# A two-branch attention kernel: last-token queries and keys in whole kilobytes, early stores of first operands, and the tail's products in other PSUM banks

## The chip, the cores and the metric

The kernel runs on one core of a Trainium2 chip. The metric is the device time of one execution in microseconds (us). The kernel before takes 1713.68 us (median of 3 runs, 1711.49 to 1714.44). All runs told here are timed beside runs of the kernel before on the same chip. The chip was not always the same: e1 to e4 ran on one, e5 to e11 on a second, e12 on a third, e13 and e14 on a fourth, so between these groups the ratios to before are compared, not the times alone.

## The reference, cut to what matters

Two attentions over the same x (2048 tokens of 576) are mixed by a gate.

```python
def _A_ref(x, mem0, Wq, Wk, Wv, Wo, seg_len):      # 32 heads of 128, segments of 32, memory of 8
    mem = mem0
    for s in range(n_seg):                          # 64 segments, one after the other
        h = jnp.concatenate([mem, xs], axis=1)      # 40 tokens: memory, then the segment
        ...                                         # q, k, v from h; masked softmax; o
        mem = o[:, :M, :].copy()                    # the next segment needs this
        outs.append(o[:, M:, :])
...
g = _sigmoid((x * gate_w).sum(-1, keepdims=True))
a = _A_ref(x, A_mem0, A_Wq, A_Wk, A_Wv, A_Wo, A_seg_len)
b = _B_ref(x, B_wqkv, B_wo)                         # ordinary attention over 2048 tokens, 32 heads of 18
return g * a + (1 - g) * b
```

Attention A is a chain of 64 segments. Attention B, "the big attention", has no such order and is worked off in steps before and between the segments.

## The kernel before

The program has three parts. In the **front** x is transposed, B's first queries and keys are projected, A's weights are loaded, and the "last tokens" are projected: the last 8 of each segment's 40 tokens do not depend on the memory, so their q, k and v are made for 16 segments at once, stored to DRAM (qld, kld, vld) and read back by segment.

```python
def last_tokens(q, share, k=None):                  # one group of 16 segments
    ...
    store = nc.sync if share else nc.gpsimd
    xlb = fil.tile([P, NF + 2, P], BF16, name="xlb", bufs=1)
    nc.sync.dma_start(out=xlb[:, :, :].rearrange("p c t -> p (c t)"), in_=xld[q])
    for b in range(HD // 512):                      # 8 blocks of values
        ...                                         # matmuls into pv
        vl = fil.tile([P, 512], BF16, name="vl")    # fil: two buffers
        copy_out(vl[:, :], pv[:, :], share)
        store.dma_start(out=vld[q * P:(q + 1) * P, b * 512:(b + 1) * 512], in_=vl[:, :])
    for w, dstd in ((wq, qld), (wk, kld)):          # 8 blocks of queries, 8 of keys
        ...
                store.dma_start(                    # 16 runs of 64 B in each of 128 rows
                    out=dstd[q].rearrange("p (s f) -> p s f", s=SG)[:, :, 4 * b * LO:4 * (b + 1) * LO],
                    in_=vl[:, :].rearrange("p (s f) -> p s f", s=SG),
                )
```

In the **loop** each segment first loads its last tokens (`v_sb` from vld, `xl` from qld and kld, copied into place by GpSimd). In the **tail** the last group of A's rows is written and the 16 row blocks of the result are finished, each in two half blocks.

```python
def bank(k, shape, dtype, name):                    # three tiles of one PSUM bank each
    if k is None:
        k = turns[0] % 3
        turns[0] += 1
    return ps_a.tile(shape, dtype, name=name, tag=f"b{k}")

def finish(n):
    ...
    for d0 in (0, Dm // 2):                         # two half blocks
        po = bank(None, [P, 512], FP32, "po")
        ...                                         # 5 matmuls into po, then ScalarE in place
        nc.scalar.activation(out=po[:, 0:Dm // 2], in_=po[:, 0:Dm // 2], func=ACT.Copy, scale=omg[:, n:n + 1])
        nc.vector.scalar_tensor_tensor(..., in1=po[:, 0:Dm // 2], op0=ALU.mult, op1=ALU.add)
```

So the product of a half block goes from TensorE to ScalarE to VectorE in the same PSUM tile, and three such tiles are used in turn.

The softmax here doesn't subtract the row's maximum and nothing guards it: scores larger than these inputs give would overflow.

## Time and profile before

| Profiled run (span 1706.9 us) | us |
|---|---|
| first segment's projections start | 234.57 |
| from there to the first final product's ScalarE step | 1430.6 |
| from there to the end | 41.7 |
| TensorE busy | 1494.8 (88%) |

The three times add up to the span; every run below is split at the same two marks (first record of the segment projections; first ScalarE step of the final products), which I call **front**, **loop** and **tail**. The loop is bound by TensorE. The front has holes in which the engines wait for a DMA for most of the time, and the tail ends in a chain of small stores. The prediction below shows the lines that carry this.

### The profile page before, as it was taken

The page shows a single profiled execution, that of the slowest core. Times are in us where ns is not written, and L with a number is a line of the kernel's source. Part 1 is how long each engine was busy: PE and PEld are TensorE (multiplying, and loading weights), DVE is VectorE, ACT ScalarE, POOL GpSimd, SP SyncE. Part 2 cuts the span into 40 slices and gives each one's busy share as a digit, 9 for nine tenths or more (in the row PEclk, how much of TensorE's full clock was granted, in tenths as well). Part 3 has the DMA queues.
Part 4 walks back from the last instruction along what each step waited for, and adds up shares of the span by engine and source line. Part 5 has one row for each costly group of instructions (what it writes and reads, how often), then busy time and mean ns, then how long its engine had stood idle before and what let it go on. Part 6 is the DMA issues. An engine that isn't in the chain of part 4 may idle for free. (4 is left out here: it accounts for less than half of the span.)

```text
span 1706.9 us, 57602 instructions
## 1 busy us (share of the span) xinstructions
PE 1494.8 (88%) x25082; PEld 789.3 (46%) x25082; DVE 963.4 (56%) x2360; ACT 1138.6 (67%) x976; POOL 364.6 (21%) x716
## 2 busy tenths in 40 slices
PE   6476669989999899999999999999999989899986
PEld 3232434445555444454555444555554444444444
DVE  2133245666666566656666656666666656565654
ACT  2154335767777676766776767777777787887873
POOL 5211111122222112131313121322221212120221
PEclk9788879999999999999999999999999999999998
DMA  7875431212221111121212111121211111111133
GB/s 191 277 266 185 106 63 33 58 35 46 50 51 45 43 37 52 44 48 35 59 38 56 42 43 47 46 47 36 58 42 48 33 46 32 45 32 31 30 103 103
DMA packets 127464, 114.38 MB, mean 67 GB/s; under 512 B 62531, under 2 KB 115011, under 8 KB 125619
## 3 DMA queue, kind: packets, MB, share of 16 engines
q1 hardware_dynamic: 106395, 59.03, 13.0%
q0 software_dynamic: 19872, 49.38, 10.9%
q8 instruction: 196, 3.21, 0.8%
q10 hardware_dynamic: 944, 2.29, 0.4%
q14 instruction: 57, 0.47, 0.1%
HBM read 60.94 MB, written 36.10 MB: 57 GB/s over the span
## 5 line engine op out<-in xcount | busy, mean ns | idle before, releaser
L257 ACT ACTIVATE etb<-sb 128x2048 bf16<-128x2048 f32 x512 | 959.5, 1874 | 420.2 <-PE sb L238 420.2
L752 DVE CAST tm<-pvv 128x512 bf16<-128x512 f32 x384 | 264.1, 688 | 170.5 <-PE pvv L740 169.1
L740 PEld LDWEIGHTS <-ht 128*32 128x32 bf16 x7680 | 187.0, 97 | 184.3 <-DVE ht L876 12.6
L238 PE MATMUL sb<-qch,kch 32*128 32x512 bf16 x2048 | 204.8, 389 | 55.6 <-ACT etb L257 36.9
L222 PE MATMUL ob<-etb,vch 128*32 128x512 bf16 x2048 | 206.8, 394 | 5.4 <-DVE tq L159 5.1
L835 DVE CAST ot<-pso 128x320 bf16<-128x320 f32 x256 | 120.3, 487 | 124.3 <-PE pso L823 120.5
L629 PE MATMUL acc<-wo,ot 128*32 128x384 bf16 (+1 forms) x4096 | 158.9, 291 | 5.4 <-DVE ot L835 3.6
L740 PE MATMUL pvv<-wq_m,ht 128*32 128x512 bf16 x2048 | 135.9, 386 | 12.6 <-DVE ht L876 7.1
L740 PE MATMUL pvv<-wk_m,ht 128*32 128x512 bf16 x2048 | 134.4, 383 | 0.0
L740 PE MATMUL pvv<-wv_m,ht 128*32 128x512 bf16 x2048 | 134.1, 382 | 0.0
L238 PEld LDWEIGHTS <-kch 32*128 32x128 bf16 x2048 | 61.7, 91 | 146.5 <-issue 111.4
L685 POOL DMA_DIRECT2D a_dram<-rl x192 | 95.9, 534 | 140.3 <-DVE rl L681 136.5
L629 PEld LDWEIGHTS <-ot 128*32 128x32 bf16 x4096 | 104.6, 97 | 45.8 <-DVE ot L835 11.6
L842 POOL COPY otl<-ot 128x256 bf16<-128x256 bf16 x64 | 27.1, 424 | 392.6 <-DVE ot L835 358.9
L222 PEld LDWEIGHTS <-vch 128*32 128x32 bf16 x2048 | 52.7, 93 | 123.7 <-issue 117.3
L293 DVE CAST vl<-pv 128x512 bf16<-128x512 f32 x96 | 65.9, 686 | 73.7 <-DMA qld<-vl 18.6
L823 PE MATMUL pso<-et,v_sb 64*128 64x40 bf16 x2048 | 82.0, 179 | 22.7 <-DMA v_sb<-tm 11.8
L811 ACT ACTIVATE lt<-pss 128x320 f32<-128x320 f32 x128 | 55.9, 437 | 68.0 <-PE pss L807 58.0
L823 PEld LDWEIGHTS <-v_sb 64*128 64x128 bf16 x2048 | 62.9, 93 | 72.5 <-issue 49.0
L767 PE MATMUL pt<-ident,tm 128*128 128x128 bf16 x1024 | 95.7, 221 | 0.8 <-DVE tm L752 0.8
L640 DVE CAST hl<-acc 128x384 bf16<-128x384 f32 (+1 forms) x128 | 57.7, 451 | 56.2 <-PE acc L629 55.9
L775 DVE COPY kt<-pt 128x512 bf16<-128x512 bf16 x128 | 53.8, 420 | 63.0 <-PE pt L767 63.0
(136 smaller groups left out, 1886.9 us busy)
## 6 DMA issues: line engine op xcount, KB each, us to landing
v_sb<-tm SPq DMA_DIRECT2D x512, 32.0 KB
wo<-in_A_Wo_dram POOLq DMA_DIRECT2D x4, 1152.0 KB, 8.1
vgd<-vt SPq DMA_DIRECT2D x32, 128.0 KB
wv_m<-in_A_Wv_dram POOLq DMA_DIRECT2D x4, 1024.0 KB, 8.1
wq_m<-in_A_Wq_dram POOLq DMA_DIRECT2D x4, 1024.0 KB, 8.2
wk_m<-in_A_Wk_dram POOLq DMA_DIRECT2D x4, 1024.0 KB, 9.1
v_sb<-vld SPq DMA_DIRECT2D x128, 32.0 KB
xl<-qld SPq DMA_DIRECT2D x64, 64.0 KB
```

What stands on the lines that cost most here:

```text
L222: nc.tensor.matmul(ob[32 * j:32 * j + 32, :], lhsT=vc[:, o + 32 * j:o + 32 * j + 32], rhs=et4[:, j, :], start=(kb == 0), stop=(kb == NKB - 1),
L238: nc.tensor.matmul(sb[:, j, :], lhsT=kc[32 * j:32 * j + 32, o:o + P], rhs=qch[gq][32 * j:32 * j + 32, :], start=True, stop=True, tile_posi ...
L257: nc.scalar.activation(out=before[:, :, :], in_=sb[:, :, :], func=ACT.Exp, scale=scale_b)
L293: nc.vector.tensor_copy(out=out, in_=in_)
L629: nc.tensor.matmul(acc[32 * j:32 * j + 32, 0:d1 - d0], lhsT=o[:, h, 0:CT], rhs=wo[:, h, d0:d1], start=(b == 0 and i == 0), stop=(b == 1 an ...
L640: nc.vector.tensor_copy(out=hl[:, 0, d0:d1], in_=acc[:, 0:d1 - d0])
L685: nc.gpsimd.dma_start(out=rows4[m, seg - LO:seg, i * n:(i + 1) * n], in_=rl[32 * i + m * LO:32 * i + (m + 1) * LO, :],)
L740: nc.tensor.matmul(pv[32 * j:32 * j + 32, :], lhsT=ht[:, cc, :], rhs=rw, start=(c == 0), stop=(c == NF), tile_position=(0, 32 * j),)
L752: nc.vector.tensor_copy(out=sbt[x][:, :], in_=ps[x][:, :])
L767: nc.tensor.transpose(out=pt[:, which, :, :, :].rearrange("p j (u i) t -> p j u i t", i=4)[:, :, :, i, :], in_=sbt[x][:, i * Dh:(i + 1) * Dh],
L823: nc.tensor.matmul(pso[:, i * L:(i + 1) * L], lhsT=v_sb[64 * jj:64 * jj + 64, b * 1024 + i * Dh:b * 1024 + (i + 1) * Dh], rhs=et[64 * jj:6 ...
L835: nc.vector.tensor_copy(out=ot[:, j * HG:(j + 1) * HG, :].rearrange("p h t -> p (h t)"), in_=ps["o", b, jj][:, 0:W8],)
```

## The change

Its intent is to close the holes of the front, to make the stores of last-token queries and keys cheaper at the price of reading small pieces ahead of time, and to let the 32 final half blocks run without a break.

```diff
-    qld = dpool.tile([n_seg // SG, P, SG * H * LO], BF16, name="qld")
+    qld = dpool.tile([n_seg // SG, H // 4, P, SG * 4 * LO], BF16, name="qld")
 ...                                       # kld likewise
-                store.dma_start(out=dstd[q].rearrange(...)[...], in_=vl[:, :].rearrange(...))
+                store.dma_start(out=dstd[q, b], in_=vl[:, :])
+                if w is wk and b == H // 4 - 1:
+                    load_xlb(q + 1)                   # the next group's tokens, a group ahead
 ...                                       # in the loop over the four blocks t of x:
+        if t == 0:
+            load_xlb(0)
+        if t < NQC - 1:
+            in_turn(next(pieces))                     # one weight piece between x blocks
         for blk in FIRST:
             project_qk(blk, t, 2)
+        if t == NQC - 1:
+            for blk in FIRST:
+                store_qk(blk, (0,))                   # before the last value projections
 ...
+    load_first()                                      # B's first operands
+    ready.extend([first_loads[-1]] * 2)               # the other weights wait for them
+    for d in pieces:
+        in_turn(d)
 ...                                       # in the loop of segments:
+            if name == "S1" and s + 1 < n_seg:
+                load_qk(s + 1)                        # 64 B pieces, a segment ahead
 ...                                       # finish(n):
-            po = bank(None, [P, 512], FP32, "po")
+            po = pf[:, (2 * n + (d0 > 0)) % 4, :]
 ...                                       # tail: group rows before the products
+    pf = ps_bs.tile([P, 4, QC], FP32, name="sb")      # one tile of four banks
+    g0 = group_span(1, 0)
+    g1 = group_span(2, 1)
+    gr = group_rows(0, n_seg - 1)
+    g0()
+    g1()
+    gl = group_last(1, n_seg - 1)
+    finish(0)
+    gr()
+    gl()
+    for n in range(1, 6):
+        finish(n)
 ...
```

The big attention's score tile, four banks wide, is free by then; the final products take its place. Half of the last group's twelve small stores go to the sync queue.

More of the change, by code (lines that the diff above doesn't have):

```diff
@@ L88 @@
     xld = dpool.tile([n_seg // SG, P, (NF + 2) * P], BF16, name="xld")
-    qld = dpool.tile([n_seg // SG, P, SG * H * LO], BF16, name="qld")
-    kld = dpool.tile([n_seg // SG, P, SG * H * LO], BF16, name="kld")
+    qld = dpool.tile([n_seg // SG, H // 4, P, SG * 4 * LO], BF16, name="qld")
+    kld = dpool.tile([n_seg // SG, H // 4, P, SG * 4 * LO], BF16, name="kld")
     aw1 = ctx.enter_context(tc.tile_pool(name="aw1", bufs=1))
@@ L197, in load_kv @@
             vch[g, kc] = bint.tile([P, KC * P], BF16, name="vch", bufs=6)
-            loads.dma_start(
+            first_loads[:] = [loads.dma_start(
                 out=vch[g, kc][:, :].rearrange("p (k f) -> p k f", f=P),
                 in_=vgd[kc * KC:(kc + 1) * KC, :, g * P:(g + 1) * P].rearrange("k p f -> p k f"),
-            )
+            )]
         def load_q(i):
@@ L260, in b_steps @@
         late.extend(divisions(ob, GB * NQC - 1))
-        while late:
-            late_part()
-    loads = nc.sync
+    loads, first_loads = nc.sync, []
     bgen = b_steps()
@@ L293, in copy_out, with load_xlb @@
             nc.vector.tensor_copy(out=out, in_=in_)
+    xlbs = {}
+    def load_xlb(q):
+        if q < n_seg // SG:
+            xlbs[q] = fil.tile([P, NF + 2, P], BF16, name="xlb", bufs=1)
+            nc.sync.dma_start(out=xlbs[q][:, :, :].rearrange("p c t -> p (c t)"), in_=xld[q])
     def last_tokens(q, share, k=None):
@@ L299, in last_tokens @@
         store = nc.sync if share else nc.gpsimd
-        xlb = fil.tile([P, NF + 2, P], BF16, name="xlb", bufs=1)
-        nc.sync.dma_start(out=xlb[:, :, :].rearrange("p c t -> p (c t)"), in_=xld[q])
+        xlb = xlbs.pop(q)
         for b in range(HD // 512):
@@ L328, in last_tokens @@
                 )
-                store.dma_start(
-                    out=dstd[q].rearrange("p (s f) -> p s f", s=SG)[:, :, 4 * b * LO:4 * (b + 1) * LO],
-                    in_=vl[:, :].rearrange("p (s f) -> p s f", s=SG),
-                )
+                store.dma_start(out=dstd[q, b], in_=vl[:, :])
+                if w is wk and b == H // 4 - 1:
+                    load_xlb(q + 1)
                 yield
@@ L455 @@
     FIRST = (0, 4, 5)
+    pieces = [(w, src) for w, src in ((wv, A_Wv), (wq, A_Wq), (wk, A_Wk))]
+    pieces = (d for w, src in pieces for d in load_weights(w, src))
     for t in range(NQC):
@@ L463 @@
         )
+        if t == 0:
+            load_xlb(0)
+        if t < NQC - 1:
+            in_turn(next(pieces))
         for blk in FIRST:
             project_qk(blk, t, 2)
+        if t == NQC - 1:
+            for blk in FIRST:
+                store_qk(blk, (0,))
         for kb in range(4 * t, 4 * t + 4):
             project_vb(0, kb, 2)
-    for blk in FIRST:
-        store_qk(blk, (0,))
-    for w, src in ((wv, A_Wv), (wq, A_Wq), (wk, A_Wk)):
-        for d in load_weights(w, src):
-            in_turn(d)
+    load_first()
+    ready.extend([first_loads[-1]] * 2)
+    for d in pieces:
+        in_turn(d)
     pgs = ps_bo.tile([P, NT], FP32, name="pgs", tag="ob")
@@ L499, in between @@
             b_advance(1)
-    load_first()
     for blk in FIRST:
@@ L684, in rest @@
                 for m in range(4):
-                    nc.gpsimd.dma_start(
+                    eng = nc.sync if s3 == n_seg - 1 and m % 2 else nc.gpsimd
+                    eng.dma_start(
                         out=rows4[m, seg - LO:seg, i * n:(i + 1) * n],
@@ L974, in load_last @@
     def load_last():
+        while late:
+            late_part()
         nc.vector.memset(wol, 0.0)
@@ L1012, in finish, with load_qk @@
         nc.sync.dma_start(out=out_td[n * P:(n + 1) * P, :], in_=ofin[n])
+    xls = []
+    def load_qk(s):
+        sq, si = divmod(s, SG)
+        w = 4 * LO
+        for srcd in (qld, kld):
+            xl = seg2.tile([P, H, LO], BF16, name="xl")
+            nc.sync.dma_start(
+                out=xl[:, :, :].rearrange("p (b h) t -> p b (h t)", h=4),
+                in_=srcd[sq, :, :, si * w:(si + 1) * w].rearrange("b p f -> p b f"),
+            )
+            xls.append(xl)
+    load_qk(0)
     for s in range(n_seg):
@@ L1016 @@
             put_x(s + 1)
-        sq, si = divmod(s, SG)
         for jj in range(2):
@@ L1023 @@
             )
-        for dst, srcd in ((qt, qld), (kt3, kld)):
-            xl = seg2.tile([P, H, LO], BF16, name="xl")
-            nc.sync.dma_start(
-                out=xl[:, :, :].rearrange("p h t -> p (h t)"), in_=srcd[sq, :, si * H * LO:(si + 1) * H * LO]
-            )
-            nc.gpsimd.tensor_copy(out=dst[:, :, CT:L], in_=xl[:, :, :])
+        for dst in (qt, kt3):
+            nc.gpsimd.tensor_copy(out=dst[:, :, CT:L], in_=xls.pop(0)[:, :, :])
         width = 8 if s >= n_seg - eights else 7
@@ L1045 @@
         assert not todo
-    n = NT - 1
-    for m in range(n):
-        finish(m)
-        if m == 2:
-            r = group_rows(None, n_seg - 1)
-        if m == 3:
-            r()
-        if m in (4, 6):
-            r = group_span(None, m // 2 - 2)
-        if m in (5, 7):
-            r()
-        if m == 9:
-            r = group_last(None, n_seg - 1)
-        if m == 10:
-            r()
-            load_rows(n)
-    finish(n)
+    pf = ps_bs.tile([P, 4, QC], FP32, name="sb")
[10 more added lines that the diff above has]
+        finish(n)
+    while late:
+        late_part()
+    load_rows(NT - 1)
+    for n in range(6, NT):
+        finish(n)
     actx.close()
```

## The prediction

> **What bounds the kernel now.** I read the page first (busy share in 40 slices), then the busy time in chosen stretches, the waits of the first 250 us, the DMA view of one stretch, and last the chain of waits that ended last with the timeline of the last 50 us.
>
> ```profile
> PE   6476669989999899999999999999999989899986
> PEclk9788879999999999999999999999999999999998
> DMA  7875431212221111121212111121211111111133
> ```
>
> A digit is a slice of 42.7 us. From the seventh slice to the last but one TensorE is busy over 90%: the loop of 64 segments (234 to 1659 us, some 22 us each) is bound by TensorE, and the 40 us stretches inside it show 36 to 38.9 busy. What can be won lies in the first six slices and the last one. Stretches of the first part (length, busy time of each engine, granted clock, DMA share, GB/s):
>
> ```profile
> 62.00:70.00 8.00, 0.00 (x0) 0.00 (x0) 0.00 (x0) 0.00 (x0) 0.70 (x3) 0.62 0.93 350
> ...
> 113.00:123.00 10.00, 1.50 (x12) 0.91 (x9) 1.11 (x3) 1.83 (x1) 1.04 (x2) 0.78 0.78 260
> ...
> 146.00:160.00 14.00, 0.54 (x2) 0.27 (x3) 0.69 (x1) 0.45 (x1) 2.71 (x3) 0.62 0.79 262
> ...
> 184.00:212.00 28.00, 17.10 (x200) 13.18 (x199) 5.07 (x8) 7.53 (x5) 3.02 (x6) 0.79 0.52 97
> ```
>
> Three holes in which no engine computes while the DMA is 78 to 93% busy, and one stretch in which TensorE works 17.1 of 28 us. The waits of the first 250 us (total, times, longest) name them:
>
> ```profile
> DVE stg L293 <- DMA qtd<-stg: 25.1, 1, 25.1
> ...
> DVE vl L293 <- DMA qld<-vl: 18.6, 7, 3.1
> ...
> PE sb L238 <- DMA kch<-ktd: 15.9, 1, 15.9
> ...
> PE pv L306 <- DMA xlb<-xld: 13.5, 1, 13.5
> ...
> DVE vt L293 <- DMA vgd<-vt: 12.4, 2, 11.3
> ```
>
> First: TensorE stops at 58.7 us and makes its first score group of the big attention at 74.67, when kch has landed; then VectorE waits until 82.62 for a stg buffer whose stores were issued behind those loads. Second (113 to 122): stores of vgd. Third: xlb, issued at 150.59 behind stores and beside the load of wo, lands at 159.4. Fourth: each VectorE copy to vl waits until the store of an earlier vl has landed. At the end, two steps of the chain that ended last, and the longest wait of the last stretch:
>
> ```profile
> 1698.10 0.50 POOL a_dram L685
> ...
> 1700.54 2.27 DMA wk_m<-a_dram
> ```
>
> ```profile
> POOL a_dram L685 <- DVE rl L681: 35.9, 1, 35.9
> ```
>
> TensorE runs the final products (L994) from 1663.4 to 1698.9. Only after eleven of sixteen row blocks is rl made (1692.0); its 12 stores, issued one by one by GpSimd, take 5.94 us; then row block 15 is read back, and the span ends at 1706.9.
>
> **What the Trainium skill says.** "DMA: Bandwidth & Descriptors", Specifications, gives 512 B as the least transfer for line rate. The trace agrees: stores of the same 128 KB from GpSimd land in 2.2 us with whole rows (vld) and in 4.5 us in 64 B pieces (qld):
>
> ```profile
> vld<-vl POOLq DMA_DIRECT2D x24, 128.0 KB, 2.2
> qld<-vl POOLq DMA_DIRECT2D x24, 128.0 KB, 4.5
> ```
>
> The same page, "Issuing engines are not separate DMA queues", says that issuing from a second engine saves only the time to issue. The 12 stores of rl are such time: 0.50 us each. "TensorE: Matmul & The Clock Gate", Part 1, says that TensorE runs at half clock until it has been busy for a few microseconds. Here the same group of four score matmuls takes 0.61 us after the hole (74.67) and 0.40 us at 88.40: a hole costs a little more than its length.
>
> **The change part by part.**
>
> *Early stores and loads of first operands.* The stores of group 0 move ahead of the last value projections on the sync queue, and the remaining 15 weight pieces wait until the first loads have landed; three pieces go out between the x blocks. Today the nine stores are issued from 55.57 to 65.5, beside two 1 MB weight pieces (DMA share 0.93), kch is issued at 70.2 and lands 4.5 us later. After: the copies that feed the stores end at 50.6 to 52.8; nine stores at about 0.65 us reach 57, four vgd stores 59, the loads go out at 59 to 60.5, and the first is there at about 62 to 63. The stores that free stg follow at 63 to 66 instead of 74.6 to 77, so VectorE gets its buffer near 70 and not 82.6. About 13 us off the path. Against it: the load of xlb for group 0 sits on the sync queue before the next x loads and waits for xld (28.2 plus 3.3 us), and the stretch from 28 to 45 us already has a DMA share of 0.80 to 0.91; I take 2 us back. Minus 11.
>
> *xlb a group ahead.* Takes out the 13.5 us at 146 to 159; but the vld stores then run beside wo, whose four loads take about 8 us each to land, so I count 2.5 us back. Minus 11. For the second group the load was also waited for, at 254.5 us, for 6.2 us. Minus 6. The other two waits total 0.9 us.
>
> *Whole kilobytes stored.* In the first group the eight qld copies start from 183.55 to 212.12, 3.57 us apart; the eight vld copies (161.81 to 183.55) are 2.72 us apart with whole rows beside the same DRAM copies. 8 x 0.85 = 6.8 us. The kld copies are already 2.2 us apart, nearer to TensorE's own pace; with warmer clock I add 1. Minus 8. Later groups: GpSimd's stores land 2.3 us sooner, inside a loop bound by TensorE: nothing.
>
> *Small pieces read a segment ahead.* Each segment's two loads change from 2 x 128 rows of 512 B to 2 x 1024 pieces of 64 B. What pieces cost, from the DMA view of 184 to 232 us, where 16 stores of 2048 pieces ran:
>
> ```profile
> q1 hardware_dynamic: 34277, 2.72, 43.7%
> ```
>
> 0.437 x 48 us x 16 engines / 34277 = 9.8 ns per piece, so an estimate of 2048 x 9.8 / 16 = 1.25 us of all engines per segment of 22 us, whose DMA share is 0.11 to 0.26 today. The gain is small: GpSimd waited 82.6 us in all for xl, but the copies into qt and kt came at about 0.4 us into the segment and the scores that need them 7 us later, so none of it is on TensorE's path. Plus 2 for collisions.
>
> *Tail.* The last divisions (2.8 us of VectorE from 1659.1) leave the front of hl; TensorE's 3.3 us wait for hl goes, and both spans of group rows (1.48 + 0.84 us) run in its place, so the final products still start at about 1664.5 (their otd loads land about then). Then 32 half blocks back to back. In the last undisturbed stretch (1693.7 to 1698.6) VectorE does 8 in 4.91 us, 0.614 each, TensorE 0.63. 32 x 0.635 = 20.3; plus 1.5 for the last ScalarE and VectorE steps, plus 2.5 from last issue to end as now: 1664.5 + 24.3 = 1688.8 against 1706.9, 18 us. rl's stores now go out around 1672 to 1676 behind four oseg stores, and row block 15 is back at about 1680, before it is wanted at 1683. For slow clock and the divisions put back after block 5 I take off 3. Minus 15.
>
> *Sum.* -11 - 11 - 6 - 8 + 2 - 15 = -49; 3 back because the weights still end near 126 us while the work that meets them is earlier (the vgd hole may grow). -46: 1713.7 - 46 = 1668.
>
> **Rivals.** *The DMA is the bound of the first part.* For: shares of 0.8 to 1.0 from 54 to 113 us, and every byte stays. The holes would then move: kch earlier, vgd or vl later. Against: from 123 to 146 the share is 0.51 and 0.19, so there is room. It would leave some 10 us of the 30 in front: 1685 to 1690. *The 64 B reads hurt the loop.* In the some 30 segments with eight score steps (65 less the 35 done before the loop), the new loads go out between the two sets of v_sb stores, and TensorE already waits now and then for v_sb (11.8 us in all). If a read piece costs three times the written one, 2 us in each of 30 segments gives 60 us back: 1700 to 1730. Against: the last v store is issued about 4.5 us after the loads, and the DMA is 80% idle there. *The tail waits elsewhere:* sync has 16 output stores and now ten more in order; if block 15 comes late, 5 us of the tail are lost, 1673. *All parts in full:* -57, 1657.
>
> **Range and chances.** The tail is the surest; the front may give 15 to 36 us; the loop may take 0 to 10. Low 1652, high 1685. Faster by over 2% means under 1679.4, which holds even with 12 us of the expected gain missing: 0.80. Same 0.18, slower 0.02.
>
> **What would show it.** First score group at 62 to 65 us; no wait of TensorE for xlb; vl copies at most 2.8 us apart throughout the first group; first segment's projections near 204 instead of 234.6; packets of queue q1 near 190 thousand (106395 - 16384 + 131072 - 30720) with the DMA share in the loop up by 0.05 to 0.1; unchanged 22 us per segment and waits of pso for v_sb under 20 us; final products at 0.62 to 0.7 us per half, span end less than 27 us after their start, the chain ending in them instead of a_dram. I am wrong if the segments lengthen, or if the first segment starts later than 215 us.

## The result, and the profile after

The changed kernel takes 1741.08 us (median of 4 runs, 1733.87 to 1744.94): slower, against 1713.53 us for the kernel before in the same rounds. The ratio is 1.0158, with a 95% interval of 1.0123 to 1.0192: clear of noise. Here and below a ratio is the mean time of one kernel's runs over that of the other's of the same rounds, so it is not quite the ratio of the medians quoted.

At the two marks the profiled runs split so:

| us | front | loop | tail | span |
|---|---|---|---|---|
| before | 234.6 | 1430.6 | 41.7 | 1706.9 |
| after | 222.9 | 1437.1 | 79.2 | 1739.1 |
| difference | -11.7 | +6.5 | +37.5 | +32.2 |
| predicted difference | -27 | -4 | -15 | -46 |

(The predicted front is -11 for the first operands, -11 for xlb, -8 for whole kilobytes and 3 back; the loop is -6 and +2.) The page of the changed kernel shows the tail at a glance; a slice is now 43.5 us:

```profile
PE   5767689989998999999998899999999998989855
PEclk9798889999999999999999999999999999999965
DMA  7785322121221121221212121212221122111320
```

In the last two slices TensorE is busy half of the time, at a granted clock of 0.6 and 0.5, where it had 8 and 6 tenths at 0.9 and 0.8 before. The waits from 1640 us on (total, times, longest) say why:

```profile
ACT sb L1014 <- PE sb L1007: 68.2, 32, 7.5
DVE wv_m L1017 <- ACT sb L1014: 58.5, 31, 2.0
...
PE sb L1007 <- DVE wv_m L1017: 34.5, 31, 1.2
```

Each engine waits for the one before it, and TensorE waits for VectorE 31 times, once for each half block after the first. The timeline shows one round (start, duration, then engine, operation and tiles; in brackets the idle time before and what ended it):

```profile
1672.20 1.36 PE L1007 MATMUL sb<-wq_m 128*128 128x288 bf16 x5 [1.11 <-DVE wv_m L1017]
...
1673.60 0.48 ACT L1014 ACTIVATE sb<-sb,omg 128x288 f32<-128x288 f32 x1 [2.00 <-PE sb L1007]
1674.10 0.51 DVE L1017 SCALAR_TENSOR_TENSOR wv_m<-wk_m,gsb,sb 128x288 bf16<-128x288 bf16 x1 [1.96 <-ACT sb L1014]
1674.67 1.36 PE L1007 MATMUL sb<-wq_m 128*128 128x288 bf16 x5 [1.11 <-DVE wv_m L1017]
```

Nothing overlaps: 1.36 us of TensorE, then ScalarE, then VectorE, then the next half block, 2.47 us from start to start. The next half block writes another bank, and still waits for the VectorE step of this one. In the kernel before, undisturbed half blocks start every 0.62 to 0.65 us, without a wait (each line has four of a half block's five matmuls):

```profile
1693.66 0.66 PE L994 MATMUL po<-wq_m,wk_m 128*128 128x288 bf16 x4
...
1694.31 0.65 PE L994 MATMUL po<-wq_m,wk_m 128*128 128x288 bf16 x4
```

In the changed kernel the first three half blocks, at full clock, take TensorE 0.78 to 0.79 us each, 1.88 to 1.97 us from start to start. From the fourth on it takes 1.36 us because its clock is down; the stretch from 1680 to 1700 us, in the columns of the prediction's table of stretches, shows it:

```profile
1680.00:1700.00 20.00, 11.10 (x43) 5.75 (x41) 5.93 (x14) 3.80 (x8) 0.00 (x0) 0.50 0.09 31
```

In the front the same stretches as before read:

```profile
62.00:70.00 8.00, 7.83 (x115) 5.33 (x114) 2.21 (x6) 1.57 (x4) 2.12 (x4) 1.00 0.64 199
70.00:78.00 8.00, 2.77 (x9) 0.83 (x10) 0.00 (x0) 1.88 (x1) 0.50 (x1) 0.72 0.77 208
113.00:123.00 10.00, 5.42 (x36) 2.81 (x36) 2.04 (x6) 3.75 (x2) 1.46 (x3) 0.76 0.98 354
146.00:160.00 14.00, 8.11 (x50) 2.99 (x50) 2.64 (x5) 6.52 (x4) 2.72 (x3) 0.96 0.77 256
184.00:212.00 28.00, 15.76 (x231) 11.88 (x231) 8.71 (x15) 11.26 (x6) 3.53 (x7) 0.97 0.35 127
```

TensorE is busy from 62 to 70 us, where it stood before, and mostly stands from 70 to 78 us instead (busy for 2.77 of 8); it works through much of 146 to 160 us. The first score group comes at 73.37 us, only 1.3 us earlier than before (74.67). The waits of the first 250 us name what took the time, first the longest of the sync queue on one DMA, then those of VectorE:

```profile
SPq L298 <- DMA xld<-xL: 23.6, 1, 23.6
```

```profile
DVE vt L291 <- DMA vgd<-vt: 27.8, 4, 8.2
DVE vl L291 <- DMA vld<-vl: 23.6, 6, 9.7
...
DVE vl L291 <- DMA qld<-vl: 15.9, 8, 2.1
```

The load of xlb stands on the sync queue until its data is stored, 23.6 us, and the x rows behind it are late. Later VectorE waits 27.8 us for vgd (12.4 before) and 23.6 us for vld. The waits of TensorE for xlb are gone. In the DMA part the queue of the sync engine has the expected packets:

```profile
q1 hardware_dynamic: 190459, 59.05, 15.4%
```

### The profile page after: what moved, and what is told of

Same layout as the page of the kernel before. It is cut to its first block, busy times and chain, and to the rows that moved or that the text cites. A ratio compares the mean times of both kernels' runs of the same rounds, so it can differ in the third digit from the quotient of the medians.

```text
span 1739.1 us, 57629 instructions
## 1 busy us (share of the span) xinstructions
PE 1518.8 (87%) x25060; PEld 796.2 (46%) x25082; DVE 963.5 (55%) x2360; ACT 1139.0 (65%) x976; POOL 330.7 (19%) x710
## 3 DMA queue, kind: packets, MB, share of 16 engines
q1 hardware_dynamic: 190459, 59.05, 15.4%
## 4 chain that ended last, share of the span: by engine, by line
PE 65%; DVE 11%; ACT 11%; DMA 9%; issue 2%; SPq 2%; DVEq 0%; POOL 0%; ACTq 0%
PE pvv L751 26%; ACT etb L257 8%; PE sb L238 7%; PE ob L222 6%; PE pt L778 5%; PE pv L323 3%; PE psh L796 3%; DMA ktd<-stg 3%; PE acc L639 2%; PE sb L1007 2%; PE pso L834 2%; DVE hl L653 2%; DVE hl L650 2%; PE pv L310 2%; DVE ot L846 1%
## 5 line engine op out<-in xcount | busy, mean ns | idle before, releaser
L751 PEld LDWEIGHTS <-ht 128*32 128x32 bf16 x7680 | 187.0, 97 | 185.8 <-DVE ht L887 12.4
L222 PE MATMUL ob<-etb,vch 128*32 128x512 bf16 x2048 | 207.7, 395 | 4.7 <-DVE tq L159 4.7
L639 PEld LDWEIGHTS <-ot 128*32 128x32 bf16 x4096 | 106.0, 98 | 46.9 <-DVE ot L846 12.4
L291 DVE CAST vl<-pv 128x512 bf16<-128x512 f32 x96 | 65.9, 686 | 63.3 <-DMA vld<-vl 23.6
L834 PEld LDWEIGHTS <-v_sb 64*128 64x128 bf16 x2048 | 63.0, 93 | 82.3 <-issue 49.5
```

The costliest lines, as they stand in the source:

```text
L222: nc.tensor.matmul(ob[32 * j:32 * j + 32, :], lhsT=vc[:, o + 32 * j:o + 32 * j + 32], rhs=et4[:, j, :], start=(kb == 0), stop=(kb == NKB - 1),
L291: nc.vector.tensor_copy(out=out, in_=in_)
L639: nc.tensor.matmul(acc[32 * j:32 * j + 32, 0:d1 - d0], lhsT=o[:, h, 0:CT], rhs=wo[:, h, d0:d1], start=(b == 0 and i == 0), stop=(b == 1 an ...
L751: nc.tensor.matmul(pv[32 * j:32 * j + 32, :], lhsT=ht[:, cc, :], rhs=rw, start=(c == 0), stop=(c == NF), tile_position=(0, 32 * j),)
L834: nc.tensor.matmul(pso[:, i * L:(i + 1) * L], lhsT=v_sb[64 * jj:64 * jj + 64, b * 1024 + i * Dh:b * 1024 + (i + 1) * Dh], rhs=et[64 * jj:6 ...
```

## The experiments

| Run | Median, range (us) | Ratio to before, 95% | front / loop / tail (us) |
|---|---|---|---|
| e1_own_banks | 1687.21, 1683.54 to 1690.37 | 0.9829, 0.9802 to 0.9856 | 226.8 / 1436.6 / 25.0 |
| e2_four_tiles | 1687.86, 1682.01 to 1693.25 | 0.9839, 0.9803 to 0.9876 | 225.7 / 1440.7 / 24.0 |
| e3_tail_undone | 1702.41, 1700.64 to 1705.82 | 0.9927, 0.9905 to 0.9949 | 220.2 / 1435.3 / 45.4 |
| e4_one_tile_before | 1755.68, 1755.22 to 1757.06 | 1.0237, 1.0217 to 1.0257 | 241.2 / 1430.3 / 82.3 |
| e5_xlb_behind | 1681.81, 1680.98 to 1691.80 | 0.9828, 0.9798 to 0.9858 | 215.3 / 1438.7 / 25.1 |
| e6_weights_free | 1681.75, 1680.84 to 1687.69 | 0.9825, 0.9801 to 0.9849 | 220.2 / 1434.1 / 25.0 |
| e7_no_pieces_between | 1681.71, 1675.73 to 1689.14 | 0.9816, 0.9784 to 0.9848 | 221.3 / 1441.0 / 25.0 |
| e8_old_layout | 1695.77, 1692.54 to 1705.58 | 0.9906, 0.9873 to 0.9938 | 233.4 / 1436.5 / 25.0 |
| e9_two_tiles_of_two | 1694.28, 1690.66 to 1702.81 | 0.9893, 0.9856 to 0.9931 | 223.0 / 1436.2 / 35.0 |
| e10_six_vl | 1672.93, 1663.77 to 1678.08 | 0.9757, 0.9719 to 0.9795 | 207.7 / 1442.1 / 25.1 |
| e11_six_vl_wo_later | 1671.08, 1670.31 to 1676.18 | 0.9762, 0.9741 to 0.9783 | 204.7 / 1438.7 / 25.0 |
| e12_pads_in_loop | 1659.12, 1655.94 to 1662.97 | 0.9660, 0.9632 to 0.9689 | 193.9 / 1442.3 / 25.0 |
| e13_loads_late | 1651.57, 1635.85 to 1655.94 | 0.9614, 0.9580 to 0.9649 | 192.4 / 1432.8 / 25.0 |
| e14_loads_at_start | 1646.54, 1643.19 to 1652.74 | 0.9610, 0.9584 to 0.9637 | 189.6 / 1426.9 / 25.1 |

By the 2% rule e10 to e14 are "faster", e4 is "slower", e5 and e7 are "unclear" and the others "same"; every interval lies clear of 1. The kernel before had medians of 1716.06 us beside the first four, 1713.81 beside the next four, 1714.23 beside e9 to e11, 1714.47 beside e12 and 1714.28 beside the last two. All results were correct. The fronts of kernels that differ only in the tail spread from 220 to 227 us, so a difference of some 5 us in one profiled front means nothing. The loops of the twelve kernels that load queries and keys in mid-segment spread by as much, from 1434 to 1442 us; only the tail is steadier. The group spans (2.3 us) stand before the second mark in the changed tail and after it in the tail of before.

### The tail: e1 to e4 and e9

My theory: the kernel's waits are made by PSUM tile, and `pf` is one tile, so its four banks give no room. The rival: the order of the new tail, or the banks themselves, is slow.

**e1_own_banks** puts the products back into the three one-bank tiles, and for that moves the group rows, which use the same tiles, ahead of the first product.

```diff
-            po = pf[:, (2 * n + (d0 > 0)) % 4, :]
+            po = bank(None, [P, 512], FP32, "po")
 ...
-    pf = ps_bs.tile([P, 4, QC], FP32, name="sb")
 ...
-    finish(0)
     gr()
     gl()
+    finish(0)
```

> The changed kernel, with the products of a half block in a tile of their own, one bank, three taken in turn, and the group's two copies put before the first half block. One-tile theory (TensorE waits for VectorE's step of the half block before because all four banks are one tile): TensorE's waits for VectorE in the final products fall from 34.5 us to under 5, the 32 half blocks take 20 to 26 us instead of 77, and the time is about 1741 - 53 = 1688 (1682 to 1695). Order theory (the new order of the tail and the divisions put back slow it): the half blocks still take over 40 us and the time stays above 1705.

Measured: 1687.21 us, faster than before. The only wait of TensorE for VectorE in the final products that is left, from the waits after 1640 us, and the step of the chain that ended last:

```profile
PE po L1007 <- DVE wv_m L1017: 1.7, 1, 1.7
```

```profile
1673.81 10.86 PE po L1007 x85
```

85 matmuls are 17 half blocks, 0.639 us each: TensorE sets the pace again. It does not yet tell tiles from banks.

**e2_four_tiles** keeps the changed kernel's order and its four banks, and only cuts them into four tiles.

```diff
-            po = pf[:, (2 * n + (d0 > 0)) % 4, :]
+            k4 = (2 * n + (d0 > 0)) % 4
+            po = ps_f.tile([P, QC], FP32, name="po", tag=f"f{k4}")
 ...
-    pf = ps_bs.tile([P, 4, QC], FP32, name="sb")
+    sctx.close()                                  # frees the score tile
+    ps_f = ctx.enter_context(tc.tile_pool(name="ps_f", bufs=1, space=psum))
```

> The changed kernel in its own order, in the four banks of sb, but cut into four tiles of one bank. One-tile theory: as e1, about 1688 (1680 to 1695); the banks are the same as in the changed kernel, so if the banks themselves or the order were the cause, the time would stay above 1730.

Measured: 1687.86 us and a tail of 24.0 us, where the same order and the same banks took 79.2 us as one tile. The banks and the order are cleared; the division into tiles is what cost.

**e3_tail_undone** gives the changed kernel the whole tail of before.

```diff
-            po = pf[:, (2 * n + (d0 > 0)) % 4, :]
+            po = bank(None, [P, 512], FP32, "po")
 ...                                              # the group rows again between the products,
 ...                                              # the last divisions and all 12 stores of rl
 ...                                              # where the kernel before has them
```

> The changed kernel with the whole tail of before: what front and loop give by themselves. From the traces: first segment 12 us earlier, 63 segments 3 us longer, so 1713.5 - 9 = 1704.5 (1700 to 1709). A theory in which the small pieces cost the loop more than the trace shows says 1713 or more.

Measured: 1702.41 us. So the front and the loop of the change are worth 0.7%, and the tail in its own tiles (e1 against e3) another 15.2 us by medians. (Its tail of 45.4 us is 3.7 us longer than the same tail in the kernel before. Only 0.8 us of that lies before the last VectorE step; from the end of that step, after which only the last output store is issued, to the end of the span it is 6.0 us here and 3.1 before. Why is not shown.)

**e4_one_tile_before** does the opposite: the kernel before, with its old order, and the products in one tile of four banks.

```diff
-            po = bank(None, [P, 512], FP32, "po")
+            po = pf[:, (2 * n + (d0 > 0)) % 4, :]
 ...
+    pf = ps_bs.tile([P, 4, QC], FP32, name="sb")
```

> The kernel before, with only the final products put in one tile of four banks. One-tile theory: a half block takes 1.9 to 2.5 us, so the 32 take 60 to 80 us instead of 35.5, and the time is 1740 to 1757. Order theory: the old order with another place for the sums stays within 10 us of before, under 1724.

Measured: 1755.68 us, and the same wait:

```profile
PE sb L994 <- DVE wv_m L1004: 31.3, 29, 1.2
```

Two lines in the kernel before cost 2.4% by themselves.

**e9_two_tiles_of_two** is the dose between: two tiles of two banks, used in turn.

```diff
-            po = pf[:, (2 * n + (d0 > 0)) % 4, :]
+            k4 = 2 * n + (d0 > 0)
+            po = pf[k4 % 2][:, k4 // 2 % 2, :]
```

> The changed kernel, only the final products put in two tiles of two banks each, used in turn, so that a half block shares its tile with the one two before it. Theory (waits are taken by tile, so the distance to the last half block in the same tile sets the pace): with one tile of four banks TensorE, ScalarE and VectorE follow one another, 2.47 us per half block; at a distance of two, a half block may run beside the ScalarE and VectorE steps of the one before, so the pace is half of such a chain, about 1.0 to 1.2 us, 32 to 38 us for 32, TensorE still waiting for VectorE nearly every time: 1696 to 1706. Rival (only a single shared tile hurts, two are as good as four): 0.64 per half block, 1684 to 1691, TensorE's waits for VectorE under 4 us.

Measured: 1694.28 us and a tail of 35.0 us, between 25 and 79. The timeline has pairs of half blocks:

```profile
1664.08 1.40 PE L1009 MATMUL po<-wq_m 128*128 128x288 bf16 x10 [0.49 <-DVE wv_m L1019]
...
1665.97 1.40 PE L1009 MATMUL po<-wq_m 128*128 128x288 bf16 x10 [0.49 <-DMA a_dram<-rl]
...
1667.87 1.40 PE L1009 MATMUL po<-wq_m 128*128 128x288 bf16 x10 [0.49 <-DVE wv_m L1019]
```

Ten matmuls, two half blocks, every 1.89 us: 0.95 us per half block, a little better than expected, for TensorE takes 0.70 us of it and not 1.36: the granted clock was 0.95 from 1659 to 1692 us, where it was 0.50 with one tile (1680 to 1700 us). (The middle round is put down to a store that landed late; its gap is the same 0.49 us.) The rival, that two tiles are as good as four, falls. (The time itself missed the expected 1696 by 2 us.)

### The front: e5 to e8 and e10 to e12

e1 is the base from here on, so that the tail is out of the way.

**e5_xlb_behind** moves the load of xlb behind the first loads.

```diff
-        if t == 0:
-            load_xlb(0)
 ...
     load_first()
+    load_xlb(0)
```

> As e1_own_banks, with the first group's xlb loaded behind the first loads of the big attention instead of at the head of the sync queue. Queue theory (the sync queue stood 23.6 us for xld, so the x rows of the third and fourth block came late): third block starts near 37 us (45.0 in the changed kernel), fourth near 46 (56.8), first score group near 62 to 64 (73.4), ratio to before falls from 0.983 to about 0.977 (0.973 to 0.980). Rival, the DMA is the bound of the front: first score group earlier, but the first segment within 3 us of e1's (227) and the ratio 0.981 to 0.985.

Measured: the queue's wait of 23.6 us is gone, the first exponential comes at 65.5 instead of 72.2 us (e1), the last-token phase begins 10 us earlier, and the front is 11.5 us shorter in the profile. The medians differ by 5.4 us, but they come from two chips, and the ratios to before are the same (0.9829 and 0.9828), where 0.977 was expected; the ratio fell where the rival had it. The profiled run of e1 is its slowest of four and that of e5 its fastest, so the two profiles flatter the edit. The earlier first scores are shown; a gain in the whole time is not.

**e6_weights_free** takes the weights' wait for the first loads out again; **e7_no_pieces_between** takes the weight pieces out of the x blocks.

```diff
-    ready.extend([first_loads[-1]] * 2)          # e6
```

```diff
-        if t < NQC - 1:                          # e7
-            in_turn(next(pieces))
```

> As e5, and the remaining weight pieces no longer wait for the first loads. Theory that the held-back weights moved the hole into the vgd stores: the waits of the vt copies for vgd, 27.8 + 10.3 us in the changed kernel, fall to 12 to 15, the first score group goes back to about 68 to 72, the ratio is 0.974 to 0.981. Rival: the weights slow the first loads by as much as they gain, ratio equal to e5's within 0.002.

> As e5, and no weight pieces between the x blocks (all eighteen after the first loads). If those three pieces delay the x rows (DMA share 0.8 to 0.9 there), the first score group comes 2 to 4 us earlier than in e5; but the weights then end some 12 us later, so the vgd and vl waits grow; ratio 0.978 to 0.985. If the pieces cost the blocks nothing, the first score group stays as in e5 and the ratio is worse than e5's by 0.003 or more.

Measured: 1681.75 and 1681.71 us, no difference from e5's 1681.81. Without pieces between the x blocks (e7) the first exponential comes at 66.7 us, not earlier than e5's 65.5, and the vgd wait stays at 25.2 us: the expected 2 to 4 us were missed. Without the weights' wait (e6) it comes at 73.4 us, and the vgd wait falls further than expected. What moves is where the front waits. VectorE's waits in the first 250 us, e5 first, then e6:

```profile
DVE vt L291 <- DMA vgd<-vt: 25.5, 7, 9.9
DVE vl L291 <- DMA vld<-vl: 24.3, 8, 9.7
...
DVE stg L291 <- DMA qtd<-stg: 10.7, 1, 10.7
```

```profile
DVE vl L291 <- DMA vld<-vl: 25.4, 8, 9.6
DVE stg L291 <- DMA qtd<-stg: 24.0, 1, 24.0
...
DVE vt L291 <- DMA vgd<-vt: 5.5, 2, 4.9
```

With the weights held back, VectorE waits for vgd; with the weights let go, it waits for stg. The two waits sum to 36.2 and 29.5 us, and TensorE's wait for the first kch grows from 3.3 to 9.5 us. This fits the prediction's rival "the DMA is the bound of the first part", for the stretch up to 146 us: a hole that is filled opens elsewhere. It does not prove it, for from 54 to 146 us the mean DMA share is 0.73 in e5 and 0.71 in e6.

**e8_old_layout** is e1 with qld and kld laid out as before: 64 B pieces stored, rows of 512 B read, still read ahead.

```diff
-    qld = dpool.tile([n_seg // SG, H // 4, P, SG * 4 * LO], BF16, name="qld")
+    qld = dpool.tile([n_seg // SG, P, SG * H * LO], BF16, name="qld")
 ...                                              # kld, the store and the load to match
```

> As e1, with qld and kld laid out as before (stored in 64 B pieces, read in rows of 512 B), still read a segment ahead. Prediction's step: the qld copies of the first group go back to about 3.6 us apart (2.8 in the changed kernel), 6 us more in front; the loop loses the 3 us that the small reads cost it (1403 against 1402 to 1408 us from first to last copy): ratio 0.983 to 0.987. If small reads hurt the loop more, the ratio is under 0.981; packets of the sync queue fall from 190 thousand to about 106 thousand.

Measured: 1695.77 us, 8.6 us over e1 by medians (another chip) and 0.8% by ratios, more than the expected 0.983 to 0.987; the copies to vl take 80.6 us from the first to the last of the group (145.5 to 226.1), where they take 68.8 us in the changed kernel (147.5 to 216.3) and in e1. The profiled front is 6.6 us longer. The loop is as e1's (1436.5 and 1436.6 us), and TensorE is idle for 103.4 us of it, 106.8 in e1. So whole kilobytes stored are worth 7 to 9 us in the front. The 64 B pieces read do take time of the DMA engines (from 300 to 1600 us the sync queue's share is 14.0% in e1 and 9.7% in e8), but cost the loop nothing that shows.

**e10_six_vl** is e5 with six vl buffers for the first group. **e11_six_vl_wo_later** also issues wo's four loads, and the copies of the pads that follow them, after the first eight blocks.

```diff
+    lctx = ExitStack()
+    vlp[:] = lctx.enter_context(tc.tile_pool(name="vlp", bufs=1, side="right")), 6
     for i, _ in enumerate(last_tokens(0, 1 << 30)):
         ...
+        if i == 15:                              # e11 only
+            ...                                  # wo and the pads, moved here
+    lctx.close()
+    vlp[:] = fil, 2                              # vl from vlp[0] with vlp[1] buffers
```

> The fifth experiment's kernel, with six vl buffers in place of two for the first group of last tokens (a pool that lives only there). Theory (two buffers, each held until its store has landed, pace the last-token blocks): VectorE's waits for vld<-vl and qld<-vl fall from 24 us to under 8, the vl copies come about 1.3 to 2.2 us apart, the first segment starts at 200 to 208 instead of 216 to 220, time 1666 to 1674. Rival (the DMA is the bound: the stores land no sooner, only further behind): the vl copies run ahead, but the first segment's first copy still waits for the loads of what was stored, and starts at 212 or later; time 1678 to 1685.

> As the run before, and the four loads of wo are issued after the first eight of the last-token blocks instead of before them, so that they do not run beside the vld stores. If the DMA's load is what makes those stores late, the vl copies of the first eight blocks come closer together than in the run before, by 5 us or more in all, and the first segment starts at 196 to 204. If the buffers alone paced them, it starts within 2 us of the run before, or later, since wo then runs beside the qld and kld stores: the same time within 3 us.

Measured: 1672.93 us in e10, 9 us less than e5; the front ends at 207.7 instead of 215.3 us. Two buffers, each held until its store lands, did pace the last tokens: VectorE's waits for vld fall from 24.3 to 11.1 us (under 8 was expected) and those for qld from 16.4 us to none that the view lists. In e11 the first eight blocks are not faster (13.9 us from the first copy to the eighth, 13.5 in e10), and the time is the same within 2 us: wo's loads beside the stores were not the cause. In both, the copies of vl end by 187 us, and then a new hole opens. These are the waits of e11 from 178 to 215 us:

```profile
PE pvv L754 <- POOL ht L631: 10.9, 1, 10.9
...
POOL qtd L547 <- DMA qtd<-qtd: 10.5, 4, 3.2
POOL ktd L547 <- DMA ktd<-ktd: 10.1, 4, 3.1
PE ptm L615 <- DMA m<-in_A_mem_dram: 10.5, 1, 10.5
```

GpSimd stands in a row of DRAM copies (the pads of qtd and ktd), which it issues two in flight and waits for one by one, until 201 us. TensorE meanwhile waits 10.9 us for ht, which GpSimd makes behind them.

**e12_pads_in_loop** leaves the first pair of these copies there and issues the other six pairs one pair in each of the first six segments.

```diff
-            for g in range(1, GB):
+            for g in range(1, 2):
                 for t in (qtd, ktd):
                     in_turn(nc.gpsimd.dma_start(out=pads(t, g), in_=pads(t, 0)))
 ...
+            if name == "S1" and s < GB - 2:
+                for t in (qtd, ktd):
+                    nc.gpsimd.dma_start(out=pads(t, s + 2), in_=pads(t, 0))
```

> The eleventh experiment's kernel; of its fourteen copies of the pads of qtd and ktd, which GpSimd issues two in flight and waits for one by one (from 162 to 201 us), only the first two stay; the other twelve are issued two in each of the first segments. Theory (with the last tokens done at 183 us, the next hole, 183 to 204 us, is GpSimd standing in that queue: TensorE waits 11 us for ht, which GpSimd copies only after the last pad copy and its constants): the first segment's kt copy comes at 192 to 197 instead of 205.2, TensorE's wait for ht falls under 3 us, time 1658 to 1664. Rival (the first segment waits for the loads of what was stored in any case, xl and m, and for wo): kt copy at 200 or later, time 1667 to 1672.

Measured: 1659.12 us, 12 us less than e11 (17 by the ratios, on another chip), with GpSimd's first kt copy at 194.83 us. The first projections now wait 0.36 us for ht:

```profile
193.90 1.90 PE L754 MATMUL pvv<-wq_m,ht 128*32 128x512 bf16 x16 [0.36 <-POOL ht L631]
```

### The loop: e13 and e14

The loop had grown in every run that reads queries and keys ahead, e8 among them, and TensorE's waits for v_sb over the whole run had gone from 11.8 us to 20 to 25 us. Piece size being excluded by e8, I suspected the place of the loads on the sync queue: in the middle of a segment, in front of the stores of the values into v_sb. **e13_loads_late** issues them near the segment's end, **e14_loads_at_start** at the start of their own segment, as before; both are e12 otherwise.

```diff
-            if name == "S1" and s + 1 < n_seg:    # e13
+            if name == "h0" and s + 1 < n_seg:
                 load_qk(s + 1)
```

```diff
+        load_qk(s)                                # e14, after the loads of v_sb
         for dst in (qt, kt3):
 ...
-            if name == "S1" and s + 1 < n_seg:
-                load_qk(s + 1)
```

> The twelfth run's kernel; the loads of the next segment's queries and keys are issued near the segment's end (after the last output product) instead of in its middle. Theory (in the middle they stand in front of the stores of the values into v_sb on the sync queue and delay them): TensorE's waits for v_sb fall from 25.0 us to 14 or less, the time from the first segment's projections to the first final product falls from 1442 to 1430-1436, the run from 1659 to 1648-1654. Rival (the v_sb waits come from something else, the value stores of the next group or the big attention's loads): v_sb waits 19 us or more, 1440 to 1444, 1656 to 1662.

> The twelfth run's kernel; the loads of queries and keys stand at the start of their own segment, as in the kernel before, in the new layout with small pieces. Theory (place on the queue): v_sb waits 14 us or less, 1430 to 1437 us from the first projections to the first final product, and the same within 3 us as the run before, because GpSimd's copies are needed only 7 us later; the first segment starts up to 2 us later. Rival: v_sb waits 19 us or more and 1440 to 1444.

Measured: 1651.57 and 1646.54 us. The loop falls from 1442.3 to 1432.8 and 1426.9 us. TensorE's waits for v_sb from 240 to 1600 us, in e12, e13 and e14 in turn:

```profile
PE pso L837 <- DMA v_sb<-tm: 19.8, 14, 3.3
```

```profile
PE pso L837 <- DMA v_sb<-tm: 12.0, 12, 2.0
```

```profile
PE pso L837 <- DMA v_sb<-tm: 13.0, 14, 2.0
```

In that stretch it is 11.8 us in the kernel before. Over the whole run the waits are 25.0, 17.0 and 17.5 us, so the expected 14 was missed there; the rest lies in the first and last segments. So the place of the loads is what made the waits for v_sb grow. How it delays the stores, by the loads' time on the queue or by the DMA's work, is not shown.

These waits explain only a part of the loop's length. The loop of each profile, from mark to mark (length, then TensorE's busy time; columns as in the prediction's table of stretches), for the kernel before, the changed one, e12, e13 and e14:

```profile
234.57:1665.20 1430.63, 1323.06 (x23695) 693.20 (x23696) 878.97 (x2195) 1041.18 (x861) 304.38 (x602) 0.99 0.18 45
222.87:1659.93 1437.06, 1331.39 (x23757) 697.53 (x23770) 879.24 (x2192) 1041.58 (x861) 273.22 (x602) 0.98 0.20 45
193.90:1636.18 1442.28, 1335.14 (x23771) 698.22 (x23772) 879.64 (x2195) 1041.30 (x862) 277.94 (x615) 0.98 0.21 47
192.37:1625.17 1432.80, 1329.66 (x23771) 697.43 (x23772) 879.23 (x2195) 1041.20 (x862) 279.68 (x615) 0.98 0.21 47
189.56:1616.42 1426.86, 1324.65 (x23771) 696.05 (x23772) 879.44 (x2195) 1041.19 (x862) 284.01 (x616) 0.99 0.21 47
```

From the kernel before to the changed one TensorE's idle time (length less busy time) did not grow, 107.6 and 105.7 us: other waits fell by as much as those for v_sb rose. It was busy for 8.3 us more. Some 2 us of that are the group spans; the trace's clock record has half clock for 48.6 us of the loop, 38.0 before, an estimated 5 us of lost work (half of the 10.6 us more). From e12 to e14 the idle time falls by 4.9 us and the busy time by 10.5, with 57.3 and 30.0 us at half clock; in e13 the idle time is 103.1 us and half clock takes 43.4.

So about a third of the loop's gain in e14 is waiting; the rest is busy time, and goes with the clock. Whether the place of the loads drives the clock is not shown: half clock takes 40 to 68 us of the loop in the twelve runs with the loads in mid-segment, 30 to 43 in the four others. (Within one kernel, too, the time follows the clock: the six runs of e13 go from 1655.94 us at a mean clock of 0.973 to 1635.85 at 0.984.) The intervals of e13 and e14 overlap or just meet e12's, so the gain of 8 to 13 us by medians is not clear of noise.

Reading ahead, the point of that part of the change, gained nothing: e14, which does not read ahead, is as fast as e13 or faster. e14 is 3.9% faster than the kernel before.

## Why the prediction was wrong

**The step that failed is the tail's "Then 32 half blocks back to back", at 0.635 us each.** It was taken from a stretch in which three tiles of one bank were used in turn, and carried over to one tile of four banks. I read the four banks of `pf` as four buffers. The runs showed a series of TensorE, ScalarE and VectorE, 1.9 us per half block at full clock and 2.47 us at half clock, and a tail of 79.2 us instead of 25. Of the error of 73 us (1741 against 1668) this is 54 us. None of the rivals named it: "the tail waits elsewhere" looked at the output stores. The diff had shown it: the argument of `finish` changed from a tile that a function hands out to a slice of one tile. With the tiles mended, 0.639 us per half block and a gain of 15.2 us came out, against 0.635 us and 15 us in the prediction.

**A third of that loss goes with the clock.** Of the 1.83 us that a half block took too long (2.47 against 0.64), 0.57 us came after the first rounds, which took 1.9 us. With an idle gap of 1.1 us in every round the granted clock stayed at 0.50 to the end, and TensorE's own part went from 0.78 to 1.36 us.

**First operands: "about 13 us off the path" was mis-sized.** The first scores came at 73.4 us and not at 62 to 65 us, for the load of xlb held up the sync queue for 23.6 us. I had seen that load and counted 2 us. But with it moved away (e5, first exponential at 65.5 us), e6 and e7 show that time saved there is given back to vgd or stg, as the rival "the DMA is the bound" has it for this stretch. I had put down 3 us of the path for a growing vgd hole; VectorE's wait there grew by 15.4 us (12.4 to 27.8), of which the path felt an unknown part. (The prediction's "holes in which no engine computes" were not quite that: in the second, TensorE was busy for 1.50 of 10 us and ScalarE for 1.83.)

**xlb a group ahead: the mechanism was right, the gain was not kept.** TensorE's wait is gone, in the second group too, and the vl copies begin 14.3 us earlier. But the eight vld stores, which I charged 2.5 us for running beside wo, then made VectorE wait 23.6 us (16.7 before), up to 9.7 at once; "at most 2.8 us apart throughout" did not hold for them. e11 shows that wo was not the reason, and e10 that it was the two vl buffers.

**Whole kilobytes: right.** The qld copies came 2.8 us apart, and e8 measures 7 to 9 us for the predicted 8.

**Small pieces: the packets and the cost of the pieces were right, the loop's length was not.** 190459 packets are the predicted 190 thousand; e8 finds no cost of the pieces in time. The DMA share in the loop rose by 0.02 (0.18 to 0.20), less than the predicted 0.05 to 0.1. Yet the loop became 6.5 us longer instead of 4 shorter. I had looked at the place of the loads and reckoned with 4.5 us to spare before the stores into v_sb; the waits for v_sb grew all the same, by 9.1 us, and fell again where the loads were moved (e13, e14). But TensorE's idle time in the loop did not grow; what grew was its busy time, by 8.3 us: some 2 us of work that was moved there from the tail, and the rest with a lower granted clock, a change that the prediction did not count. What lowered the clock stays open.

**One hole after another.** The sum of the front's parts was worked out as if each hole could be filled by itself. Every hole filled showed the next one: kch, vgd, the vl buffers, GpSimd's row of pad copies. The predicted start of the first segment, 204 us, was reached only in e11, with three repairs that the change does not have (xlb behind the first loads, six vl buffers, wo later); e14 is at 189.6 us. What stays open is how much of VectorE's vgd and stg waits, still 25.7 and 12.1 us in e10, could be had without moving fewer bytes.

## What to carry to other kernels

Count buffers by what the waits are made on, the tile, and not by the banks or bytes in it: four banks in one tile are one buffer, and the first look at any new loop should be whether each engine waits for the last step of the round before. When a DMA, or an engine that issues DMAs, has to wait for data, everything behind it in the same program order waits too, so place loads that wait last, and leave engines that are needed soon free of long rows of them. A rate measured with one set of buffers is not a rate for another. And before a longer loop is put down to a wait that grew, compare the bounding engine's idle and busy time: here one wait grew by 9 us and the idle time by nothing.

## What the Trainium skill lacked or had wrong

- "PSUM — Partial Sum Buffer", section on bank collisions, has the rule to guard PSUM by bank and quadrant, with the bank as the simple form. That is for what the hardware needs; no page says that a kernel's waits may be made by whole tile. Here a half block that writes another bank of the same tile waited every time: 79.2 us of tail with one tile of four banks, 35.0 with two of two, 24.0 with four of one.
- "DMA: Bandwidth & Descriptors", Specifications, gives one least size for line rate, 512 B, and does not tell stores from loads. Here 64 B pieces cost the kernel time in stores (7 to 9 us for 16 stores of 128 KB in the front, e1 against e8). Read, 2048 pieces per segment, they raised the sync queue's DMA share from 9.7% to 14.0% and cost the kernel nothing measurable (loops of 1436.5 and 1436.6 us): the stores were waited for, the loads were not.
- The same page, "Issuing engines are not separate DMA queues", says that a second issuing engine saves only the time to issue. That section does not say that the issuing engine's other work waits with it (the page's section on the anatomy of one DMA, which puts semaphore waits on the issuing sequencer, implies it): GpSimd's row of pad copies held the first segment for 10.9 us (e11), and its removal was worth 12 us (e12); one load on the sync queue held later loads for 23.6 us.
